# Sliding-window attention: scores in 32x64 tiles, five half-key slots to a block of keys instead of six

## The chip, the cores and the metric

The kernel runs on one core of a Trainium2 chip. Times are device microseconds (us) of whole executions, medians of a handful of runs. A profile is one execution taken by the hardware profiler; its span is some 2 us shorter than the time of that execution. In this kernel TensorE does the matrix products, ScalarE the exponentials, GpSimd the masks, VectorE sums and inverses; `PSUM` is the memory to which TensorE's products go. Code and diffs are cut to the lines that matter (`...` marks most cuts), and some comments in them are added.

## The reference

Two independent problems of the same shape, whose outputs are laid side by side:

```python
# x: 2048 x 1024, wqkv: 1024 x 3072, wo: 1024 x 1024, all bf16
H = 32; Dh = 32; W = 256
qkv = (x @ wqkv).reshape(B, S, 3, H, Dh)          # ... to q, k, v by heads
scores = einsum("bhqd,bhkd->bhqk", q, k) * Dh ** -0.5
mask = (i_q - i_k >= 0) & (i_q - i_k < W)         # causal, the last 256 keys
p = softmax(where(mask, scores, -1e9))
out = einsum("bhqk,bhkd->bhqd", p, v) ... @ wo
```

A block of 128 keys is seen by queries of its own block (the diagonal, masked to a triangle), of the next (all of it), and of the one after (the far edge, the other triangle).

## The kernel before

Four heads of 32 make a head group of 128 rows, as many as the widest products of the traces have (128*128). The work is cut into *sessions*. A session computes the scores of four 128x128 blocks for each of four heads into one tile of 128x2048 in PSUM (`st`), takes one exponential of 128x2048 on ScalarE (`pt`), and masks diagonals and far edges in place on GpSimd. Scores use TensorE as four row tiles of 32x128.

```python
def session(now):
    es = entries_of(now)                           # SLOTS = 4 blocks (group, keys j, queries q)
    st = ps_st.tile([P, 4, SLOTS, P], F32, name="st")
    ...                                            # a:b = blocks of the same keys
            for r in range(4):
                nc.tensor.matmul(
                    st[:, r, a:b, :],
                    lhsT=kT[32 * r:32 * r + 32, j * P:(j + 1) * P],
                    rhs=qT[32 * r:32 * r + 32, q * P:(q + b - a) * P],
                    start=True, stop=True, tile_position=(32 * r, 0))
    ...
    nc.scalar.activation(out=pt[...], in_=st[...], func=ACT.Exp, bias=-SHIFT, scale=cfg.scale)
    for a, (g, j, q) in enumerate(es):
        blk = pt[:, :, a, :]
        if q == j:                                 # diagonal: affine_select in place
        elif q == j + 2:                           # far edge: affine_select in place
```

Once the blocks that two blocks of queries need are done, `edge` adds a diagonal and a far edge into one tile (`both`) on VectorE, and `pv` multiplies the weights by the values, and by a tile of ones for the denominators, in four column tiles of 128x32. VectorE then takes the inverse, spreads it and multiplies.

```python
def pv(g, p):
    ...
    for x, (h, j, o, w_, src) in enumerate(moves):
        for r in range(4):
            nc.tensor.matmul(acc[32 * r:32 * r + 32, o:o + w_], lhsT=lhsT, rhs=src[:, r, :, :],
                             start=(x == 0), stop=(x == len(moves) - 1), tile_position=(0, 32 * r))
```

The projections (q and k, V, output) fill the rest of TensorE's time, a few steps after each session. A step is one product of 128x128 weights with 512 columns (256 for V). In a session that has pv, the steps too are cut into four column tiles, so that the array keeps its shape (in the traces a change of it takes 0.096 us, see the balance below); otherwise they use the whole array:

```python
def by_columns(out, lo, hi, lhsT, rhs, start, stop):
    if whole[0]:                                   # one matmul of 128x128
        nc.tensor.matmul(out[:, lo:hi], lhsT=lhsT, rhs=rhs, start=start, stop=stop, ...)
        return
    for c in range(0, P, 32):                      # four matmuls of 128x32, side by side
        nc.tensor.matmul(out[c:c + 32, lo:hi], lhsT=lhsT[:, c:c + 32], rhs=rhs, start=start,
                         stop=stop, tile_position=(0, c), skip_group_check=True)
```

Each matmul is two instructions, a weight load and the product. So a step takes two instructions on the whole array and eight in column tiles, for the same time: in the trace before, steps of 512 columns start 0.216 us apart and steps of 256 columns 0.109, either way.

## Time and profile before

| | before |
|---|---|
| time, median of 3 runs | 609.52 us (609.34 to 609.76) |
| span of the profile | 607.6 us |
| TensorE | 98% busy, 96% of the chain that ended last |
| sessions | 180, each one exponential of 1.878 us |
| matmuls of TensorE | 12,837, each with a weight load (the page has 12,838 loads: the one f32 product at the end is recorded twice) |

The prediction shows the lines on TensorE. Two lines of the page that it doesn't show matter below: the queue that brings instructions, and the group of the exponentials. The first has packets, MB, and share of the DMA engines' time. The second has busy us, mean ns of one, and the idle time before them.

```profile
q8 instruction: 102, 1.67, 1.2%
...
L459 ACT ACTIVATE pt<-st 128x2048 bf16<-128x2048 f32 x180 | 338.0, 1878 | 91.6 <-PE st L451 73.5
```

1.67 MB in 102 packets are 16,384 bytes each. Taking 256 instructions to a packet (the distance of the stops found below), that is 26,112 in all. TensorE issues 2 x 12,837 = 25,674 loads and products, so I read this queue as TensorE's program, brought in as it runs.

### The profile page before, as it was taken

The page shows a single profiled execution, that of the slowest core. Times are in us where ns is not written, and L with a number is a line of the kernel's source. Part 1 is how long each engine was busy: PE and PEld are TensorE (multiplying, and loading weights), DVE is VectorE, ACT ScalarE, POOL GpSimd, SP SyncE. Part 2 cuts the span into 40 slices and gives each one's busy share as a digit, 9 for nine tenths or more (in the row PEclk, how much of TensorE's full clock was granted, in tenths as well). Part 3 has the DMA queues.
Part 4 walks back from the last instruction along what each step waited for, and adds up shares of the span by engine and source line. Part 5 has one row for each costly group of instructions (what it writes and reads, how often), then busy time and mean ns, then how long its engine had stood idle before and what let it go on. Part 6 is the DMA issues. An engine that isn't in the chain of part 4 may idle for free.

```text
span 607.6 us, 28768 instructions
## 1 busy us (share of the span) xinstructions
PE 593.6 (98%) x12786; PEld 344.3 (57%) x12838; DVE 468.4 (77%) x1199; ACT 441.1 (73%) x376; POOL 326.3 (54%) x630
## 2 busy tenths in 40 slices
PE   8999999999999999999999999999999999999996
PEld 6555466656655756564556756655455665545443
DVE  1677889898898898897888887898888887897200
ACT  3778887788888887877778877777776777785332
POOL 0565666665666666556555565555555655554000
PEclk9999999999999999999999999999999999999999
DMA  9833110111015501442111100112021040113222
GB/s 234 182 92 89 37 38 3 38 38 39 3 38 90 114 14 30 82 101 77 38 37 38 38 4 8 33 37 81 2 68 34 4 106 21 55 58 120 72 79 64
DMA packets 86802, 35.47 MB, mean 58 GB/s; under 512 B 65552, under 2 KB 86160, under 8 KB 86672
## 3 DMA queue, kind: packets, MB, share of 16 engines
q1 hardware_dynamic: 85632, 33.31, 22.2%
q8 instruction: 102, 1.67, 1.2%
q10 hardware_dynamic: 1040, 0.26, 0.2%
q14 instruction: 28, 0.23, 0.1%
HBM read 17.83 MB, written 8.39 MB: 43 GB/s over the span
## 4 chain that ended last, share of the span: by engine, by line
PE 96%; ACT 2%; issue 1%; DMA 1%; ACTq 0%
PE pp L176 44%; PE pp L172 28%; PE acc L513 13%; PE st L451 10%; ACT pt L459 1%; DMA oT<-in_A_x_dram 1%; PE acc L582 0%; PE pp L568 0%; ACT kT L190 0%; ACT vt L190 0%; PE st L582 0%; ACT osb L190 0%; PE pp L805 0%; ACTq L190 0%
## 5 line engine op out<-in xcount | busy, mean ns | idle before, releaser
L459 ACT ACTIVATE pt<-st 128x2048 bf16<-128x2048 f32 x180 | 338.0, 1878 | 91.6 <-PE st L451 73.5
L471 POOL TENSOR_SCALAR_AFFINE_SELECT pt<-pt 128x512 bf16<-128x512 bf16 x224 | 154.5, 690 | 145.7 <-ACT pt L459 143.1
L467 POOL TENSOR_SCALAR_AFFINE_SELECT pt<-pt 128x512 bf16<-128x512 bf16 x256 | 179.2, 701 | 85.8 <-ACT pt L459 85.8
L524 DVE RECIPROCAL rinv<-acc 128x128 f32<-128x128 f32 x128 | 122.0, 953 | 57.0 <-PE acc L513 56.4
L176 PE MATMUL pp<-xT,wqk 128*32 128x512 bf16 x2712 | 163.1, 379 | 0.0
L481 DVE TENSOR_TENSOR both<-pt 128x512 bf16<-128x512 bf16 x224 | 137.1, 651 | 0.0
L176 PEld LDWEIGHTS <-wqk 128*32 128x32 bf16 x2712 | 69.3, 97 | 54.2 <-issue 0.4
L172 PE MATMUL pp<-xT,wqk 128*128 128x512 bf16 (+1 forms) x323 | 76.7, 369 | 4.1 <-issue 2.4
L176 PE MATMUL pp<-wv,xT 128*32 128x256 bf16 x2436 | 75.9, 273 | 0.0
L451 PE MATMUL st<-qT,kT 32*128 32x384 bf16 (+2 forms) x1488 | 71.5, 269 | 0.1
L176 PEld LDWEIGHTS <-xT 128*32 128x32 bf16 x2436 | 63.8, 97 | 6.2
L529 DVE STREAM_SHUFFLE wide<-rinv 128x128 f32<-128x128 f32 x256 | 64.6, 298 | 0.0
L513 PE MATMUL acc<-pt,vt 128*32 128x128 bf16 (+1 forms) x2160 | 63.3, 239 | 0.0
L172 PE MATMUL pp<-wo_sb,oT 128*128 128x512 bf16 (+1 forms) x269 | 59.3, 373 | 1.3 <-issue 0.9
L451 PEld LDWEIGHTS <-kT 32*128 32x128 bf16 x1488 | 22.2, 92 | 64.5 <-issue 63.3
L190 ACT CAST osb<-pp 128x512 bf16<-128x512 f32 (+1 forms) x52 | 30.0, 577 | 39.1 <-PE pp L172 24.4
L531 DVE TENSOR_TENSOR oT<-acc,wide 128x256 bf16<-128x256 f32 x128 | 54.3, 425 | 4.4
L176 PE MATMUL pp<-wo_sb,oT 128*32 128x512 bf16 x952 | 55.6, 379 | 0.0
L172 PEld LDWEIGHTS <-wqk 128*128 128x128 bf16 x362 | 33.4, 98 | 37.0 <-issue 6.8
L172 PE MATMUL pp<-wv,xT 128*128 128x256 bf16 x415 | 50.9, 273 | 1.4 <-ACT kT L190 0.6
L513 PEld LDWEIGHTS <-vt 128*32 128x32 bf16 x2160 | 35.9, 96 | 26.4 <-issue 24.1
L172 PEld LDWEIGHTS <-xT 128*128 128x128 bf16 x415 | 38.9, 98 | 12.0 <-issue 6.1
(46 smaller groups left out, 386.5 us busy)
## 6 DMA issues: line engine op xcount, KB each, us to landing
out_dram<-osb SPq DMA_DIRECT2D x63, 128.0 KB, 1.8
wqk<-in_B_wqkv_dram SPq DMA_DIRECT2D x32, 128.0 KB, 2.5
wqk<-in_A_wqkv_dram SPq DMA_DIRECT2D x24, 128.0 KB, 2.7
wo_sb<-in_A_wo_dram SPq DMA_DIRECT2D x16, 128.0 KB, 2.2
wv<-in_B_wqkv_dram SPq DMA_DIRECT2D x16, 128.0 KB, 2.8
wo_sb<-in_B_wo_dram SPq DMA_DIRECT2D x16, 128.0 KB, 2.4
oT<-in_A_x_dram SPq DMA_DIRECT2D x4, 256.0 KB, 5.4
wv<-in_A_wqkv_dram SPq DMA_DIRECT2D x2, 512.0 KB, 5.9
```

The source lines that it names most:

```text
L172: nc.tensor.matmul(out[:, lo:hi], lhsT=lhsT, rhs=rhs, start=start, stop=stop, skip_group_check=True)
L176: nc.tensor.matmul(out[c:c + 32, lo:hi], lhsT=lhsT[:, c:c + 32], rhs=rhs, start=start, stop=stop, tile_position=(0, c), skip_group_check=True)
L190: nc.scalar.copy(out=out, in_=in_)
L451: nc.tensor.matmul(st[:, r, a:b, :], lhsT=kT[32 * r:32 * r + 32, j * P:(j + 1) * P], rhs=qT[32 * r:32 * r + 32, q * P:(q + b - a) * P], st ...
L459: nc.scalar.activation(out=pt[:, :, :n, :].rearrange("p r a q -> p r (a q)"), in_=st[:, :, :n, :].rearrange("p r a q -> p r (a q)"), func= ...
L467: nc.gpsimd.affine_select(out=blk, in_=blk, pattern=[[0, 4], [1, P]], compare_op=ALU.is_ge, fill=0.0, base=0, channel_multiplier=-1)
L471: nc.gpsimd.affine_select(out=blk, in_=blk, pattern=[[0, 4], [-1, P]], compare_op=ALU.is_gt, fill=0.0, base=0, channel_multiplier=1)
L481: nc.vector.tensor_tensor(out=both[:, :, h, :], in0=pts[s0][:, :, a0, :], in1=pts[s1][:, :, a1, :], op=ALU.add)
L513: nc.tensor.matmul(acc[32 * r:32 * r + 32, o:o + w_], lhsT=lhsT, rhs=src[:, r, :, :], start=(x == 0), stop=(x == len(moves) - 1), tile_pos ...
L524: nc.vector.reciprocal(out=rinv[:], in_=acc[:, 2 * P:3 * P])
L529: nc.vector.stream_shuffle(out=wide[:, h * P:(h + 1) * P], in_=rinv[:], mask=[16 * h] * 32)
L531: nc.vector.tensor_tensor(out=oTs[(pi, k)][:, t, (p % 2) * 256:(p % 2 + 1) * 256], in0=acc[:, 0:256], in1=wide[:], op=ALU.mult)
```

## The change

A diagonal block's upper-right half is masked away, and so is the far edge's lower-left. With keys cut into two halves of 64, each half is seen by only 320 queries: five slots of 64 instead of six. The half with the earlier keys misses the last 64 queries, the other half misses the first 64, so slot 4 of the first half holds its diagonal start while the second half holds its far end (the "wrap"). A session keeps its 128x2048 exponential but now does 8/5 of a block of keys instead of 4/3. Since the wrapped slots aren't in order for pv, the mask of the diagonal copies it to a tile of its own (`diag`). The check that inputs are in range moves from |q| and |k| to the inverse denominators, at the end.

```diff
-SLOTS = 4
+SLOTS = 8
+HALF = 64
-PV_LAG = 3
+PV_LAG = 2
...
     def session(now):
...
+            lo = [x for x in range(a, b) if us[x][2] < 4]
+            hi = [x for x in range(a, b) if us[x][2] < 4 or j + 2 < NB]
...
+        for g, j, c, a, w_, q in todo:
             qT, kT = qks[g]
+            keys = slice(j * P + c * HALF, j * P + (c + 1) * HALF)
             for r in range(4):
+                rows = slice(32 * r, 32 * r + 32)
                 nc.tensor.matmul(
-                    st[:, r, a:b, :],
-                    lhsT=kT[32 * r:32 * r + 32, j * P:(j + 1) * P],
-                    rhs=qT[32 * r:32 * r + 32, q * P:(q + b - a) * P],
-                    start=True, stop=True, tile_position=(32 * r, 0))
+                    scores[c * HALF:(c + 1) * HALF, r, a * HALF:(a + w_) * HALF],
+                    lhsT=kT[rows, keys], rhs=qT[rows, q:q + w_ * HALF],
+                    start=True, stop=True, tile_position=(32 * r, c * HALF),
+                    skip_group_check=True)
...
+            nc.gpsimd.affine_select(out=diags[(g, p)][:, :, h, lo:lo + HALF],
+                                    in_=pt[:, :, a * HALF:(a + 1) * HALF], ...)
...
-                    add_or(dst)
+                nc.vector.scalar_tensor_tensor(
+                    out=top[:], in0=inverses[0][:]..., scalar=IN_RANGE, in1=top[:],
+                    op0=ALU.bitwise_xor, op1=ALU.bitwise_or)
```

`edge` and `pv` follow: their blocks come from `diag` and from runs of slots in `pt`. `by_columns` is untouched.

## The prediction

> **What bounds the kernel now.** I read the page's busy table first, then the chain that ended last, then the waits of TensorE, and then TensorE's timeline in the steady state.
>
> ```profile
> PE 593.6 (98%) x12786; PEld 344.3 (57%) x12838; DVE 468.4 (77%) x1199; ACT 441.1 (73%) x376; POOL 326.3 (54%) x630
> ...
> PE 96%; ACT 2%; issue 1%; DMA 1%; ACTq 0%
> PE pp L176 44%; PE pp L172 28%; PE acc L513 13%; PE st L451 10%; ACT pt L459 1%; DMA oT<-in_A_x_dram 1%; PE acc L582 0%; PE pp L568 0%; ACT kT L190 0%; ACT vt L190 0%; PE st L582 0%; ACT osb L190 0%; PE pp L805 0%; ACTq L190 0%
> ```
>
> TensorE holds 96% of the chain. The scores (L451) are a tenth of it; the projections (L172 whole array, L176 in four column tiles) are 72%, weights times values and denominators (L513) 13%. A busy TensorE can still hide waiting, since ends of matmuls are modelled, so I checked its waits:
>
> ```profile
> PE pp L172 <- issue: 3.5, 22, 0.2
> PE pp L568 <- DVE ones L783: 1.3, 1, 1.3
> PE pp L172 <- ACT vt L190: 1.0, 2, 0.5
> ```
>
> These are its three largest, in us in total, times, and longest. Nothing of size: TensorE isn't held up by the exponentials, masks or sums. So only a change of TensorE's own work can move the end, and time freed elsewhere is worth nothing by itself. The timeline gives the price of that work, from start to next start:
>
> ```profile
> 303.79 0.82 PE L176 MATMUL pp<-xT,wqk 128*32 128x512 bf16 x12
> 304.44 1.70 PE L176 MATMUL pp<-wv,xT 128*32 128x256 bf16 x56
> 306.07 0.40 PE L451 MATMUL st<-qT,kT 32*128 32x256 bf16 x8
> 306.40 0.39 PE L172 MATMUL pp<-wv,xT 128*128 128x256 bf16 x2
> ...
> 309.10 0.40 PE L451 MATMUL st<-qT,kT 32*128 32x128 bf16 x8
> 309.43 0.51 PE L513 MATMUL acc<-pt,vt 128*32 128x128 bf16 x16
> 309.77 0.28 PE L513 MATMUL acc<-pt,ones 128*32 128x128 bf16 x8
> 309.88 0.29 PE L513 MATMUL acc<-both,ones 128*32 128x128 bf16 x8
> 309.99 2.33 PE L176 MATMUL pp<-xT,wqk 128*32 128x512 bf16 x40
> 312.25 0.40 PE L451 MATMUL st<-qT,kT 32*128 32x384 bf16 x8
> ```
>
> Three groups of four 512-column matmuls take 304.44 - 303.79 = 0.65 us, so 0.216 a group, whose pure streaming at 2.4 columns per ns (512 / 0.2133) is 0.213. Two groups of 128 take 0.11 (309.77 to 309.88): 0.056 each. Before a session of scores there is a hole: ten groups from 309.99 should end at 312.15, and the scores start at 312.25. From the scores to what follows is 0.33 us (306.07 to 306.40, 309.10 to 309.43) for 512 columns, 0.12 over streaming. From pv to projection there is no hole. So a change of the array's tile shape costs about 0.10 us, a session has two, and it costs 0.10 + 0.33 = 0.43 us, half of which is not arithmetic.
>
> As a check of the whole: projections 1512 groups of 512 x 0.216 = 326.6 and 1072 of 256 x 0.109 = 116.8; pv 856 of 128 x 0.056 and 180 of 256 x 0.109 = 67.6; scores 180 x 0.43 = 77.4. Sum 588.4 us of the 607.6 us span. The rest is the start (first scores at 13.8 us, of which some 5 is projection), the 5 us tail after the last copy, and some 5 us of small waits[...]. TensorE has no reserve to give except in its work.
>
> [...]
>
> **The change part by part.** The instruction lists of the two built programs give the counts.
>
> *Fewer sessions.* A head group needs 45 blocks of 128 keys x 128 queries now, four to a session: 16 x 45 / 4 = 180. A block of 128 keys needs five slots of 64 queries instead of six, so a head group needs 76, eight to a session: 16 x 76 / 8 = 152. The exponential stays 128x2048. ScalarE saves 28 x 1.878 = 52.6 us, off the path, and gets back some 24 copies at 0.58 = 14.
>
> *Scores on TensorE.* 372 groups in 180 sessions become 976 groups in 152: 416 of 64 columns, 120 of 128, 128 of 192, 200 of 256, 112 of 320. A frequent session issues lower half 256, upper half 320, lower 64, lower 192, upper 192. Both halves carry 512 columns, so if they run side by side a session still streams for 0.213 us. A second group of scores starts today 0.066 us after one of 128 columns and 0.173 after one of 384, 0.013 over streaming, presumably because it waits for the last of the four rows. With three or four groups in line per half that makes 0.27 to 0.30, mean 0.28 (an estimate), plus two changes of shape at 0.10: 0.48 a session. 152 x 0.48 = 73.0 against 77.4: 4.4 us saved. Were there no such row penalty, 0.43 x 152 = 65.4: 12 us saved.
>
> *pv.* Columns stay 155,648, as a diagonal block only comes from another tile; but blocks cut by a session's end make 1232 groups of 1036, 192 of them of 64 columns. 196 x 0.003 us = 0.6 us lost. If a 64-column group costs as much as a 128-column one, 192 x 0.027 = 5 us more.
>
> *Projections.* Same columns. A larger share goes in four column tiles (1734 groups against 1525), which costs nothing: 0.216 either way.
>
> *GpSimd.* 480 selects of 512 elements at 0.69 to 0.70 become 512 of 256 for the diagonal, 192 of 512 and 64 of 256 for the far edge. The identity's select has 128 elements and takes 0.292, so 256 are near 0.43: 576 x 0.43 + 192 x 0.695 = 381 against 334, up 47 us, still 2.5 us in a session of 3.9.
>
> *VectorE.* The 128 ORs of q and k (67.6 us) become 64 of the inverse denominators (some 0.53 each, 34). The 224 edge sums (137 us) become 192 plus 64 half-sized at some 0.36: 148. 24 fewer copies: 16 less. Some 39 us saved, off the path.
>
> *Order.* pv comes two sessions behind, not three, but sessions are longer (7.8 us against 10); the check of the range moves to the end with 32 projection steps, near 6.9 us, to hide it.
>
> Sum on TensorE: -4.4 + 0.6 = -3.8 us.
>
> **The rivals.** (1) The halves don't overlap. Then a session streams some 0.51 us, costs 0.71 and all 108: +30 us, 640. Against it: four column tiles and four row tiles each overlap in this trace[...]. (2) Narrow groups bound by weight loads: 416 score groups and 192 pv groups of 64 columns, each some 0.025 late, +5 to +12 us on top: 611 to 617. The trace has no group so narrow[...]. (3) No row penalty and perfect overlap: 597.5, right at -2%. (4) The masks become a wait: a sum needs a session's diagonals one session later, GpSimd ends some 5.3 us after the session's scores began, and VectorE[...] may hold copies of projections behind it. Two projection banks would then stall TensorE: +0 to +10. Against it: VectorE has a quarter of the time free. (5) The freed engines speed things up: their waits are nil in TensorE's list, so nothing.
>
> **The range and the chances.** The sum says 605.7. Case 3 seems to me somewhat likelier than 2 and 4 together, so I go to 604.5. The range is 597 (case 3) to 614 (2 or 4 in part). Faster by 2% needs under 597.3: all of case 3 and a little more, 0.14. Slower by 2% means above 621.7, case 1 or 2 and 4 together: 0.09.
>
> **What would show it.** 152 exponentials of 1.88 us; starts of scores to what follows at 0.33 to 0.40 us, not 0.60; holes of 0.10 us before the scores; 64-column pv groups 0.03 us apart; GpSimd near 370 to 390 us; no VectorE or GpSimd line of size among TensorE's waits. The prediction is wrong if a score session takes over 0.5 us from its start to the next work, or if TensorE's waits name the sums or the copies.

The sum came to -4.4 + 0.6 = -3.8 us on TensorE, so 605.7 us. Measured numbers that its arguments need: 2.4 columns per ns is the slope between its own groups, 512 - 128 columns in 0.216 - 0.056 us. The four matmuls of a group, in column tiles or in row tiles, start 2 to 5 ns apart (median 4), which is the overlap that speaks against rival 1. A second group of scores starts 0.056 us after the last of the four rows of one of 128 columns, and 0.163 after one of 384. In the first stretch of the span TensorE is slower: its first five products of 512 columns start 0.40 to 0.43 us apart instead of 0.216, at a granted clock of 1.00 by the profile. The 0.025 us in rival 2 and the 0.36 us of a half-sized edge sum were estimates, with no trace behind them; in the changed kernel's trace the 64-column pv groups start 0.029 us apart, and the half-sized sums have a mean of 0.559 us (0.616 for the full ones).

## The result

The changed kernel is correct and takes **618.72 us** (617.77 to 621.31, four runs) against 609.64 for the one before in the same rounds. The ratio is 1.0156, with a 95% interval of 1.0124 to 1.0188. Ratios here are the mean time of one kernel's runs over that of the other's of the same rounds, so not quite the ratio of the quoted medians. It is 1.5% slower: within the 2% band, but outside the predicted range of 597 to 614, and on the other side of the time before. The sign was wrong.

The page of the changed kernel, in the parts that answer to the lines shown of before:

```profile
PE 598.9 (97%) x16665; PEld 372.8 (61%) x16665; DVE 429.9 (70%) x1143; ACT 405.8 (66%) x372; POOL 372.1 (60%) x918
...
q8 instruction: 132, 2.16, 1.5%
...
PE 90%; issue 3%; POOL 2%; DMA 2%; DVE 1%; ACT 1%; SPq 0%; POOLq 0%; ACTq 0%
...
L497 ACT ACTIVATE pt<-st 128x2048 bf16<-128x2048 f32 x152 | 285.5, 1878 | 90.2 <-PE st L490 63.1
L507 POOL TENSOR_SCALAR_AFFINE_SELECT diag<-pt 128x256 bf16<-128x256 bf16 x512 | 216.3, 448 | 194.3 <-ACT pt L497 180.5
```

The intent was met: 28 exponentials fewer at the same 1.878 us, ScalarE 35 us and VectorE 39 us less busy, GpSimd at 372. But TensorE's share of the chain fell from 96% to 90%, and "issue", time in which an engine waits for nothing that the profile shows, rose from 1% to 3%. And TensorE's program has grown by 30 packets, to 132 x 256 = 33,792 instructions.

TensorE's waits say the same (us in total, times, longest), for the changed kernel:

```profile
PE acc L562 <- issue: 4.9, 10, 1.1
PE st L490 <- issue: 2.2, 3, 1.4
...
PE pp L195 <- DMA xT<-in_A_x_dram: 1.1, 1, 1.1
PE pp L199 <- issue: 0.9, 2, 0.5
```

Before, the longest wait for "issue" was 0.2 us. Now there are few, but each of up to 1.4 us, and they fall in the middle of pv and of scores. No wait for the sums or the masks is among them, and only one of 0.3 us for a copy.

The steady state, from TensorE's timeline of the changed kernel (start, length, engine, line, tiles, columns, count; neighbours of one kind are one row):

```profile
303.45 0.42 PE L490 MATMUL st<-qT,kT 32*64 32x256 bf16 x20
303.80 0.41 PE L562 MATMUL acc<-pt,vt 128*32 128x128 bf16 x12
...
308.00 1.70 PE L199 MATMUL pp<-wv,xT 128*32 128x256 bf16 x56
309.52 1.25 PE L199 MATMUL pp<-xT,wqk 128*32 128x512 bf16 x20
310.71 0.42 PE L490 MATMUL st<-qT,kT 32*64 32x192 bf16 x20
311.06 0.82 PE L195 MATMUL pp<-xT,wqk 128*128 128x512 bf16 x3
```

From the scores to what follows is 0.35 us (303.45 to 303.80, 310.71 to 311.06): with the hole of 0.10 before them, 0.455 a session, where I had predicted 0.48 and feared 0.71. So the halves do run side by side. And 14 V steps take 309.52 - 308.00 = 1.52 us, 0.109 each, as before. Where nothing stops TensorE, every part costs what was predicted, or less.

So I looked for where something stops it. The timeline of its weight loads in the changed kernel, at such places (in brackets the idle time before the row and what ended it):

```profile
208.68 0.16 PEld L562 LDWEIGHTS <-ones 128*32 128x32 bf16 x7
209.86 0.17 PEld L562 LDWEIGHTS <-ones 128*32 128x32 bf16 x9 [1.02 <-issue]
...
212.81 0.34 PEld L562 LDWEIGHTS <-vt 128*32 128x32 bf16 x27
214.41 0.09 PEld L562 LDWEIGHTS <-vt 128*32 128x32 bf16 x1 [1.26 <-issue]
```

A row of 16 loads of ones is torn after the seventh: 1.02 us of nothing. The seventh and the eighth belong to one group of four, whose products read the same tile, so it isn't a wait for data. 4.55 us later (209.86 to 214.41) it happens again, exactly 256 loads and products further on.

**All stops at one place of the instruction stream.** I numbered TensorE's loads and products in the order of their issue, and added up the holes by number modulo 256, from 16 us into the span on (worked out from the traces, in us):

```
holes of over 0.06 us by position modulo 256 (16 positions to a bin)
after : 176-191: 12.6   224-239: 0.6   32-47: 0.4   all others together: 0.4
before: none over 2.1 (32-47); 0.1 to 2.1 in most bins; 176-191: 0.4
```

In the kernel before the small holes lie anywhere (part of them are records of matmuls that are missing from its trace: it has 12,786 of 12,837). In the changed kernel nearly all is at one position, once in 256 instructions, which is one packet of the instruction queue. That the position isn't 0 is presumably due to other instructions ahead of the first load (33,792 fetched, 33,328 loads and products). In 29 of 126 blocks of 256 TensorE stops at the boundary, for 12.6 us in all; counted in the same way, from position 150 to 199, the kernel before has 2.0 us in 9 of 96. So it waits for its own program. The instruction packets are never under 3.2 us apart in the changed kernel (median 5.7 us before); at a stop the median time from the start of a fetch to the block's first instruction is 2.3 us.

The packets in the kept traces show the link directly. At the 17 stops of over 0.25 us in the changed kernel, TensorE goes on 1.2 to 1.6 us after the last instruction packet has ended (median 1.4; 1.4 too in e4, with 63 such stops). At boundaries without a stop that distance is anything from 0.1 to 8.5 us. And the packet before a stop began only 0.6 to 2.3 us after TensorE had entered the block that it then ran out of (median 1.4; in e4 after 0.35 to 3.8), and took 1.0. So at a stop no further block was in stock. The three medians add up to 3.8 us from entering a block to starting the next, an estimate that lies near the 3.5 fitted below.

By how long the block ran before its stop, the stops of the changed kernel are (blocks of up to 6.75 us):

```
block runs for (us)    2.5    3.0    3.5    4.0    4.5 and more
blocks                   3     16     40     28     36
of these with a stop     0     10     15      3      1
us of stops            0.0    5.7    6.0    0.7    0.2
```

A block that TensorE runs through in 3.75 us or less is liable to stop; of those that take 4.5 us or more, 1 in 36 did. Summing max(0, 3.5 us - duration of the block without a stop) over the blocks of the program gives 12.8 us here and 1.1 us for the kernel before. I call this the block law. 3.5 is fitted, and the law holds for sums, not for each block (three blocks of 2.5 us had no stop). It was written down after e1 to e4 had run, so what it gives for e1 and e4 is a check after the fact.

**The balance on TensorE**, from the first score to the last weight load. "Own work" is what its sequence of instructions takes without stops: columns / 2.4 + 2.5 to 2.7 ns a group of matmuls, 0.096 us a change of tile shape, and the scores of a session at 0.235 us before and 0.262 after, all measured in the two traces.

| | before | after | difference |
|---|---|---|---|
| own work | 582.9 | 575.5 | -7.4 |
| stops at block boundaries | 2.0 | 12.6 | +10.6 |
| lost otherwise | 3.1 | 6.2 | +3.1 |
| first score, after the first weight load | 12.5 | 14.5 | +2.0 |
| sum | | | +8.3 |

The spans differ by 616.0 - 607.6 = 8.4. The change does save TensorE 7.4 us, about twice what I said, and then loses 13.7 us in stops and waits and 2.0 at the start. The start, in the timeline of the changed kernel, where session 0 needs queries of the second chunk of x:

```profile
10.10 2.81 PE L195 MATMUL pp<-xT,wqk 128*128 128x256 bf16 x24
13.98 1.90 PE L195 MATMUL pp<-xT,wqk 128*128 128x512 bf16 x8 [1.08 <-DMA xT<-in_A_x_dram]
15.81 0.42 PE L490 MATMUL st<-qT,kT 32*64 32x256 bf16 x20
```

TensorE waits for x for 1.08 us, and the scores start at 15.81; before, they started at 13.83.

### The profile page after: what moved, and what is told of

The parts are those of the page before. It is cut to its first block, busy times and chain, and to the rows that moved or that the text cites. A ratio compares the mean times of both kernels' runs of the same rounds, so it can differ in the third digit from the quotient of the medians.

```text
span 616.0 us, 36878 instructions
## 1 busy us (share of the span) xinstructions
PE 598.9 (97%) x16665; PEld 372.8 (61%) x16665; DVE 429.9 (70%) x1143; ACT 405.8 (66%) x372; POOL 372.1 (60%) x918
## 4 chain that ended last, share of the span: by engine, by line
PE 90%; issue 3%; POOL 2%; DMA 2%; DVE 1%; ACT 1%; SPq 0%; POOLq 0%; ACTq 0%
PE pp L199 46%; PE pp L195 22%; PE acc L562 13%; PE st L490 9%; DMA xT<-in_A_x_dram 2%; POOL diag L507 1%; POOL pt L518 1%; DVE both L529 0%; DVE rinv L575 0%; ACT pt L497 0%; SPq L603 0%; DVE wide L580 0%; ACT osb L207 0%; DVE top L585 0%; ACT vt L207 0%
## 5 line engine op out<-in xcount | busy, mean ns | idle before, releaser
L497 ACT ACTIVATE pt<-st 128x2048 bf16<-128x2048 f32 x152 | 285.5, 1878 | 90.2 <-PE st L490 63.1
L507 POOL TENSOR_SCALAR_AFFINE_SELECT diag<-pt 128x256 bf16<-128x256 bf16 x512 | 216.3, 448 | 194.3 <-ACT pt L497 180.5
L518 POOL TENSOR_SCALAR_AFFINE_SELECT pt<-pt 128x512 bf16<-128x512 bf16 (+1 forms) x256 | 161.0, 647 | 0.0
L529 DVE TENSOR_TENSOR both<-diag,pt 128x512 bf16<-128x512 bf16 (+1 forms) x256 | 144.8, 602 | 15.1 <-POOL diag L507 11.1
L490 PEld LDWEIGHTS <-kT 32*64 32x64 bf16 x3904 | 41.1, 103 | 57.6 <-issue 57.4
L490 PE MATMUL st<-qT,kT 32*64 32x64 bf16 (+4 forms) x3904 | 66.3, 236 | 2.3 <-issue 2.2
L562 PE MATMUL acc<-pt,vt 128*32 128x128 bf16 (+2 forms) x1792 | 50.8, 224 | 1.5 <-issue 1.4
L207 ACT CAST vt<-pp 128x512 bf16<-128x512 f32 x53 | 30.9, 584 | 20.4 <-PE pp L199 14.1
L207 ACT CAST qT<-pp 128x512 bf16<-128x512 f32 x51 | 29.8, 585 | 21.5 <-PE pp L199 13.8
L195 PEld LDWEIGHTS <-oT 128*128 128x128 bf16 x269 | 25.8, 98 | 29.8 <-issue 0.8
```

What stands on the lines that cost most here:

```text
L207: nc.scalar.copy(out=out, in_=in_)
L490: nc.tensor.matmul(scores[c * HALF:(c + 1) * HALF, r, a * HALF:(a + w_) * HALF], lhsT=kT[rows, keys], rhs=qT[rows, q:q + w_ * HALF], start ...
L497: nc.scalar.activation(out=pt[:, :, :n * HALF], in_=scores[:, :, :n * HALF], func=ACT.Exp, bias=-SHIFT, scale=cfg.scale)
L507: nc.gpsimd.affine_select(out=diags[(g, p)][:, :, h, lo:lo + HALF], in_=pt[:, :, a * HALF:(a + 1) * HALF], pattern=[[0, 4], [1, HALF]], co ...
L518: nc.gpsimd.affine_select(out=blk, in_=blk, pattern=[[0, 4], [-1, w_ * HALF]], compare_op=ALU.is_gt, fill=0.0, base=-HALF * (us[a][2] - 3) ...
L529: nc.vector.tensor_tensor(out=both[:, :, h, o:o + w_], in0=dg[:, :, h, o:o + w_], in1=pts[t][:, :, a:a + w_], op=ALU.add)
```

## The experiments

The theory: TensorE's program arrives in blocks of 256 instructions, and where it runs through a block too fast, it waits for the next. The rivals: the stops belong to the code where they are seen (pv bursts, narrow groups, a wait for an edge sum that the profile doesn't show); pv being only two sessions behind; the late start. Eleven runs; all gave correct results. Ratios are against the kernel before, of the same rounds.

### e1: projection steps between the groups of pv

```diff
-        finish_norm(1)
-        pv(pg, pk)
+        finish_norm()
+        done += pv(pg, pk, now)          # pv emits one projection step after each group
```

> The changed kernel with one projection step put after each group of the values-and-denominators product, so that scores and pv no longer stand in one dense burst; same instructions, same tile shapes, same columns. Theory (instruction supply: TensorE runs dry at blocks of 256 of its own instructions when a burst empties the stock): the stops at one place of every 256 instructions fall from about 15 us to under 3 us and the time from 618.7 to 602 to 607 us, below the kernel before. Rival (masks and sums arrive late at the shorter lag): pv ends about 1.5 us later in its session, which does not help a wait before it; 615 to 621 us. Rival (narrow groups are slow by themselves): the groups are as narrow as before, 616 to 620 us.

Measured: 616.75 us against 609.99, ratio 1.0105 (1.0087 to 1.0123). This missed the 602 to 607 that my theory had asked for. Stops at the block boundary were 13.7 us, no less than in the changed kernel. (The edit also finishes all pending inverses before pv, where the changed kernel leaves one, and it ends up with 24 loads more.) What follows: thinning out the pv burst of under 100 instructions doesn't remove the stops; the column tiled steps put between them are themselves dense. The theory of the time, that a burst empties a stock, had to become one of whole blocks; by the block law e1 should stop for 14.8 us.

### e2: the same program, moved by 128 instructions

```diff
+    for _ in range(64):
+        nc.tensor.matmul(warm[:, 0:1], lhsT=blank[:, 0:P], rhs=blank[:, 0:1], start=True, stop=True)
```

> The changed kernel with 64 one-column matmuls more at the start, 128 instructions, so that every later instruction stands half a block further in the stream. Instruction supply: stops of the same kind, 8 to 20 us in sum, at the same place modulo 256 of the stream, but before other program instructions than in the changed kernel; time 614 to 622 us. Rival (a wait on data): the stops stay before the same instructions of the program, as the masks and sums have not moved; time 620 us.

Measured: 621.35 us, ratio 1.0189 (1.0172 to 1.0206). 128 instructions are half a block, so every boundary now meets other code. The stops, 14.2 us, of which 14.1 are at positions 176 to 191 again, have left pv and moved to the projections. From TensorE's waits:

```profile
PE pp L199 <- issue: 8.9, 11, 1.5
...
PE acc L562 <- issue: 0.8, 2, 0.6
```

In the changed kernel these two were 0.9 and 4.9. The code at which TensorE stops is changed by a shift, the place in the stream isn't. That rules out the rivals that tie the stops to pv, to its edge sums or to narrow groups: the stop is in the supply of instructions.

### e3: pv three sessions behind, as before

```diff
-PT_BUFS = 5          +PT_BUFS = 6
-PV_LAG = 2           +PV_LAG = 3
-edgep bufs=2         +edgep bufs=1
-osbp bufs=4          +osbp bufs=2
```

> The changed kernel with pv three sessions behind the scores instead of two (six buffers of exponentials, for which one edge buffer and two output buffers were given up). Rival (masks and sums arrive late): VectorE's idle time before the edge sums behind the masks, 11 us, disappears and the time falls by 5 us or more, to under 614. Instruction supply: the stops stay, 10 to 20 us in sum, and the time is 616 to 622 us.

Measured: 634.67 us, ratio 1.0412 (1.0395 to 1.0429). Both sides missed the time. The memory for the sixth `pt` was taken from other pools, and they became waits of their own; from all waits of this kernel:

```profile
DVE both L529 <- PE acc L562: 79.0, 54, 5.3
...
ACT osb L207 <- DMA out_dram<-osb: 15.8, 8, 3.5
```

Sums wait for pv to give back their only buffer, copies for the output's DMA. Stops at boundaries were 17.5 us. The run is inconclusive on the lag as such; it shows only that three sessions can't be had here at this price.

### e4: the kernel before, with pv in 64 columns

```diff
+        moves = [(h, j, o + HW * i, HW, src, i) for (h, j, o, w_, src) in moves for i in range(w_ // HW)]
```

> The kernel before with every pv group cut into pieces of 64 columns: same columns, 2432 groups instead of 1036, so 8 x 1396 = 11,168 instructions more, all within the burst. Instruction supply: beside 1396 x 0.003 = 4 us of group overhead, stops at one place of every 256 instructions, 10 us or more in sum, which the kernel before has not; time 622 to 640 us. Rival (data waits only): 613 to 615 us, and no stops at a fixed place of the stream.

Measured: 666.09 us against 609.99, ratio 1.0907 (1.085 to 1.0964). No half-key tiles, no `diag`, the same sessions and masks: only 11,168 more instructions for TensorE, in the same work. Its page and its waits:

```profile
PE 625.9 (94%) x18422; PEld 372.4 (56%) x18422; DVE 456.5 (69%) x1199; ACT 442.9 (67%) x376; POOL 317.3 (48%) x630
...
q8 instruction: 146, 2.39, 1.5%
```

```profile
PE pp L177 <- issue: 14.8, 20, 2.0
PE acc L515 <- issue: 9.8, 24, 0.9
```

Own work rises by only 3.6 us (586.5 from 582.9). TensorE stops 40.7 us at block boundaries, in 63 of 140 blocks; the law, applied afterwards, gives 45.8. So the stops can be made in the kernel before by instructions alone. The effect was larger than the 622 to 640 that I had written: I had sized it by the count of instructions, and it goes by how many blocks fall below some 3.5 us. In all 58.4 us are lost beyond own work, 17.7 of them not at boundaries (3.1 in the kernel before); I didn't resolve those.

### e5: V on the whole array

```diff
     def by_columns(out, lo, hi, lhsT, rhs, start, stop):
+        if hi - lo == 256:
+            whole[0] = True
         if whole[0]:
```

> The changed kernel, but a session goes over to the whole array for the rest of its projections as soon as it comes to a V step (256 columns): 2 instructions where four column tiles take 8. TensorE's instructions fall from 33,328 to 28,312, at the price of 56 more changes of tile shape, 5.6 us. Instruction supply, in the sharper form that the first runs gave (a block of 256 TensorE instructions cannot be had faster than about 3.5 us, so each block of the program that would last less stops TensorE for the difference): this sum over the program's blocks is 12.8 us in the changed kernel and 0.9 here, so 618.7 + 5.6 - 11.9 = 612.4, range 610 to 615, and stops under 3 us. Rival (the stops have to do with data, not with the stream): 624 us.

Measured: 609.65 us against 609.69, ratio 0.9999 (0.9983 to 1.0014), so 9.1 us below the changed kernel. V steps are the densest code, eight instructions in 0.109 us, so that a block of them would last 3.5 us. With two instead of eight (and the rest of that session's steps on the whole array too) the program falls to 112 packets. This costs 56 more changes of shape, own work 580.8 instead of 575.5, and stops fall from 12.6 to 1.9 us. What is left of TensorE's waits for its program:

```profile
PE pp L197 <- issue: 2.1, 13, 0.2
```

That is the answer to the main question: take away instructions, with the same arithmetic, score tiles, masks and lag, and the loss goes. The run beat my figure (610 to 615) slightly. Own work (+5.3) and stops (-10.7) make 5.4 of the 7.6 us between the two spans; the first score comes 0.5 us earlier, and what is lost otherwise falls from 6.2 to 4.2 us, for which I have no cause.

### e6: the kernel before without its ORs

```diff
-                    add_or(dst)
```

> The kernel before without its 128 ORs of q and k (67.6 us of VectorE's time); the range check then looks at zeros and passes, which is right for these inputs. If VectorE's freed time is worth nothing by itself, as predicted: 608.5 to 610.5 us. If part of the change's effect came through VectorE: outside that.

Measured: 608.02 us, ratio 0.9978 (0.9962 to 0.9993), half a microsecond below the range written. Taking 128 ORs (67.6 us) off VectorE alone gives 0.2%. So an engine off the path wasn't quite worth nothing, as the prediction's fifth rival had it, but little. The kernel serves here only as a measure: without the ORs it no longer checks its range.

### e7 and e8: column tiles only where the block can afford them

The scheduler counts the instructions it has issued and their estimated time; where the block under way would last less than 3.5 us, the steps of that session use the whole array, and sessions on the whole array prefer V. e8 also loads the second chunk of x before wv.

```diff
+        budget = level(now) - fixed[now]
+        whole[0] = whole[0] or dense(now, budget)   # block of 256 would last under 3500 ns
+        emit(now, budget)
...
+            wanted = [n for n in ready if (chains[n].steps[0][0] < 200.0) == whole[0]]
```

> The changed kernel with its projections paced by the instruction stream: V chains go to the sessions without pv where they can wait, and a session takes the whole array where a block of 256 instructions would else last under 3.5 us. 16 more changes of shape (1.6 us); the sum of shortfalls over the blocks falls from 12.8 to 0.5 us. Instruction supply: 618.7 + 1.6 - 12.3 = 608.0, range 606 to 611, and stops under 3 us. Rival: 619 to 621 us.

> The same, with the second chunk of x loaded ahead of the first V weights, because the changed kernel's first session needs its queries and TensorE waits 1.1 to 1.9 us for that load at the start. If that wait is on the path to the end: 1 to 2 us less than the paced kernel, 606 to 608 us. If the V weights then come as late: the same time as the paced kernel.

Measured: e7 609.70 us, ratio 1.0001 (0.9987 to 1.0014); e8 608.87, ratio 0.9988 (0.9975 to 1.0002). Stops are 2.5 and 3.0 us, at only 16 more changes of shape than the changed kernel (own work 577.0). So the law is good enough to steer by. e7 lies in its range; e8 is above its 606 to 608, and its 0.8 us below e7 is within the noise. The gain over e5 didn't come: where two V chains in a row run on the whole array, TensorE stands for some 0.4 us (7 holes, 3.1 us in all, in e7's and e8's traces). I put that to waits for their copies, since a chain of V is only half as long as one of q or k, and there are two buffers for them; TensorE's waits in e7 and e8 name the copies of V for 1.0 us, 4 times, so for the rest it isn't shown.

### e9 and e10: the order of the first loads alone

```diff
-    load_wv(0, 0, CT, nc.sync)
     new_x(0, 1)
     load_x(0, 1)
+    load_wv(0, 0, CT, nc.sync)
```

e9 is the changed kernel with this, e10 is e5 with this.

> The changed kernel with the second chunk of x loaded ahead of the first V weights, nothing else. If the wait for it at the start (1.1 to 1.9 us) reaches the end: 616.5 to 618 us against 618.7 for the changed kernel. If it is taken up elsewhere: 618 to 620 us.

> The V steps on the whole array (609.65 us) with the second chunk of x loaded first. 1.3 us less, as between the two paced kernels (0.8 measured there): 608.0 to 609.2 us, at or just below the kernel before.

Measured: e9 618.90 us against 609.56, ratio 1.0149 (1.0133 to 1.0164); e10 608.47, ratio 0.9986 (0.9973 to 1.0). In e9 the first score does come 2.0 us earlier (12.5 us after the first load, not 14.5), but the end doesn't move: stops at boundaries went from 12.6 to 17.7 us, in 40 blocks. In e10, where the supply isn't short, the first score comes 0.9 us earlier than in e5, and the time is 1.2 us shorter; but the two intervals overlap, so this gain is no more than likely. That the time saved in e9 turned into longer stops fits these two runs, but isn't shown: each sum of stops is from one execution.

### e11: as e8, but never two V chains in a row by choice

```diff
+            narrow = whole[0] and not last_narrow[0]
+            wanted = [n for n in ready if (chains[n].steps[0][0] < 200.0) == narrow]
```

> The paced kernel with x first, but never two V chains in a row by choice: two in a row on the whole array waited 0.4 us for their copies some seven times. 18 more changes of tile shape (1.7 us), the sum of shortfalls 0.9 us as against 0.5. If those waits were what the paced kernel lost beyond its sum: 606.5 to 608.5 us. If not: 609 to 611 us.

Measured: **607.17 us** (606.73 to 608.67) against 609.56, ratio 0.9968 (0.9954 to 0.9981), as expected. It is the fastest kernel of all: 11.5 us below the changed one, 0.3% below the one before. The holes between two V steps on the whole array, 7 with 3.1 us in e8, are down to 2 with 1.0 us. The step from e8 (1.7 us) is small beside the noise: the two intervals just overlap. Its page:

```profile
PE 589.0 (97%) x14576; PEld 362.8 (60%) x14628; DVE 429.2 (71%) x1144; ACT 405.3 (67%) x371; POOL 372.6 (62%) x918
...
q8 instruction: 116, 1.90, 1.4%
```

14,628 loads against 16,665 make 116 packets, and stops of 3.0 us. Own work is 578.7, lost altogether 6.8.

| kernel | own work | stops, by the law | stops, measured | time |
|---|---|---|---|---|
| before | 582.9 | 1.1 | 2.0 | 609.64 |
| after | 575.5 | 12.8 | 12.6 | 618.72 |
| e1 | 575.5 | 14.8 | 13.7 | 616.75 |
| e4 | 586.5 | 45.8 | 40.7 | 666.09 |
| e5 | 580.8 | 0.9 | 1.9 | 609.65 |
| e7 | 577.0 | 0.5 | 2.5 | 609.70 |

## Why the prediction was wrong

**What bounds the kernel: right, but not complete.** TensorE sets the end in both kernels. The inference "only a change of TensorE's own work can move the end" was the first gap: work is not the only thing an engine at 96% of the chain needs. It needs its instructions, and the kernel before had few blocks near the limit (seven of its blocks ran under 3.75 us). The reserve that I didn't look at was there in the page, in the line of the instruction queue.

**The sum on TensorE, -3.8 us: right in sign, low in size.** Measured -7.4. The term that was off is the session's 0.48 us: it is 0.10 + 0.355 = 0.455. The penalty for groups in line, put at 0.27 to 0.30 for the streaming of 512 columns, came to 0.26. 152 x 0.455 = 69.2 against 180 x 0.43 = 77.4 is -8.2, and the rest of the table is small.

**"A larger share goes in four column tiles (1734 groups against 1525), which costs nothing: 0.216 either way": this is the step that failed.** The time of a group is the same, as predicted, 0.216 and 0.109. But a group is eight instructions instead of two. The 209 more groups of it, with 604 more groups of scores and 196 more of pv, made 25,674 instructions into 33,328, in less time. The sum left out that this rate has a limit. It cost 10.6 us more in stops at the boundaries, more than all that the tiles saved. e2 shows that they are a matter of the place in the stream, e4 that instructions alone make them, e5 that taking instructions away removes them.

The instruction queue shows the blocks on both pages: 102 and 132 packets of 16,384 bytes, and the stops are 256 instructions apart. In the kernel before, the boundaries cost 2.0 us, in 9 of 96 blocks; in the changed one 12.6 us, in 29 of 126.

**Rival 1, halves one after the other: refuted**, by the 0.35 us from scores to what follows. **Rival 2, narrow groups bound by weight loads: refuted.** The 64-column pv groups start 0.029 us apart, little over their streaming of 0.027, although 611 to 617 was the nearest of the figures to what came: a right-looking number for a wrong reason. **Rival 3, no penalty and perfect overlap:** half right. It meant 12 us less of TensorE's work, my sum 3.8, and 7.4 came; none of it was seen in the time. **Rival 4, masks as a wait:** it exists, but costs TensorE next to nothing. In all waits of the changed kernel:

```profile
DVE both L529 <- POOL diag L507: 11.1, 25, 0.9
...
PEld L562 <- issue: 7.8, 15, 1.3
```

VectorE waits for diagonals for 11.1 us, and TensorE's waits don't name VectorE's sums or copies. The page's chain does run through GpSimd (2%) and VectorE (1%), most of it in one stretch from 91.7 to 121.5 us; but TensorE was busy for 29.4 of these 29.8 us, with one wait of 0.4 us, for "issue". **Rival 5, freed engines are worth nothing:** nearly; e6 puts it at 0.2%.

**GpSimd near 370 to 390: right**, 372.1, a select of 256 elements taking 0.448, not the 0.43 estimated. (VectorE's edge sums were put at 137 us before and 148 after, the one a busy time and the other counted from the mean of 0.651 us; like for like they would have been 141, and 144.8 came. They are off the path.) **The start was not foreseen:** I didn't ask which data session 0 needs first. It delays the first score by 2.0 us; e9 shows that mending it alone gains nothing in this kernel, and e10 suggests some 1 us where TensorE gets its program in time.

**The test that I set was too narrow.** It named a session over 0.5 us, or waits for sums and copies, as what would prove me wrong. Neither came for the reason meant: four of 152 sessions took 0.51 to 2.03 us, with a stop in their scores, and one wait of 0.3 us named a copy. The time was wrong all the same. None of the five rivals was about the supply of instructions, so the range, drawn from the rivals, was too narrow above.

**What stays open.** Why a packet begins only 0.6 to 2.3 us after the block before a stop is entered, and why 1.4 us pass between its end and TensorE's going on. Stopped blocks last 3.57 us with their stop, on average, where the DMA engines were under 20% busy (12 blocks), and 4.17 where they were busier (14 blocks), with packets that took 1.1 us in both; this is a correlation, and no run looked for its cause. The 3.1 us more that are "lost otherwise", and the 17.7 of e4, aren't resolved either.

## What to carry to other kernels

When TensorE is nearly always busy, count its instructions as well as its columns: tiling the array multiplies the instructions for the same arithmetic (eight instead of two for a step of the same 0.216 or 0.109 us), and here a block of 256 that would run in less than about 3.5 us was liable to make TensorE wait for the next. Waits for "issue" of up to 1.4 us in the middle of a burst whose data have long been there were its mark here, and numbering the stream modulo 256, or moving it by half a block, tells it from a wait of that code. Then spend tiles where they buy time (scores, pv), and use the whole array where the tiles only spare a change of shape.
